# Four head pairs' softmax sums in one group beside a projection, the inverses spread through DRAM, and a new order of transposes and loads

## The chip, the core and the metric

The kernel runs on one core of one Trainium2 chip. The metric is the device time of one execution in microseconds, lower is better. A core has a matrix engine (TensorE, PE in the profile, with its weight loads shown as PEld), a vector engine (DVE), a scalar engine (ACT), GpSimd (POOL, used here to issue loads) and SyncE (SP, used to issue stores, transposes and copies). Each engine works through its own queue in order; they wait for each other by semaphores.

## The reference

Two layers. First an attention with projected keys and values (8 batches, 8 heads, 1024 tokens, head size 64, 64 projected keys), then a feed-forward layer on its output with the square of a ReLU (512 to 2048 to 512).

```python
k_proj = np.einsum('ks,bhsd->bhkd', E, k)
v_proj = np.einsum('ks,bhsd->bhkd', F, v)
scores = scale * np.matmul(q, k_proj.transpose(0, 1, 3, 2))
attn = np.exp(scores - max) / (sum + 1e-09)
x = np.matmul(attn, v_proj)          # then heads side by side: 8192 x 512
out = np.square(np.maximum(x @ w_in, 0.0)) @ w_out
```

## The kernel before

Matmuls are in bf16. The feed-forward layer takes most of the time. Each batch is cut in two chunks of 512 tokens, and both products of a chunk are done by a scheme with seven block products in place of eight (Group for the first layer, Chunk.second_spread for the second), with the sums that it needs on DVE.

After a beginning (batch 0, loads of the weights) comes one main loop of 399 numbered steps (both, L865). A step emits one block product of the first layer (four matmuls of 256 columns, L669) and one quarter product of the second layer of the chunk before (four more, L583). F_STEPS (L833) repeats every seven steps, so a group takes 7 steps, a chunk 28, a batch 56. Steps are counted from 1; firsts of batch 1 are steps 1 to 56, those of batch 2 steps 57 to 112.

The attention of later batches is hung on these steps. on(step, b, name) puts a method of batch b's Attention behind the matmuls of a step (L871 to L901, with t = 56(b-1)+28). TensorE's order is exactly that of the program. The other engines' order is made by a planner when the program is built, from its own estimates of durations; issue_after and add_manual_dep add an order by hand.

One batch's attention consists of these pieces:

- load_kv and load_q (L243 to L248): 1 MB each after the cast to bf16, issued by POOL. K, V and Q have one buffer each, so a load waits until the former batch's tensor has been used.
- project (L266): 16 matmuls with 64 output rows, k's in rows 0 to 63 of one PSUM bank, v's in rows 64 to 127 of the other; then DVE and ACT copy them out (keep_k, keep_v).
- transpose_k_dma and transpose_q_dma (L303, L330): transposes by DMA, issued by SP. qT and kT have one buffer each.
- scores for a head pair (L362): two matmuls of 512 columns, then one Exp on ACT (L353) into one of four expT buffers.
- sums_spread for two head pairs (L386): eight matmuls of 64 rows by 32 columns with a matrix of ones (L392) give the softmax sums, each repeated over 32 rows, of both pairs; Ln and Exp(-x) on ACT (L396, L397) make the inverses; eight copies by DMA within SBUF (L403) repeat them to the 64 rows where they are needed, in two of three "rs" buffers (the third held the source).
- values for a head pair (L406): four matmuls (L415), and two multiplications by rs on DVE (L419) into xT, the input of the first layer.

All attention pieces of the main loop share one pair of PSUM banks (att_psum), so each waits until the piece before has been read out. In the steady state of the loop the order for batch b+2 is: q's transpose at t+26, projection t+28, k's transpose t+30, scores t+44, t+47, (sums t+50), t+53, t+57, (sums t+59), values t+63, t+66, t+76, t+79. K and V of batch b+3 are loaded behind k's transpose (L897), Q of batch b+2 at t+11 behind the last values queued so far (L891). Stores of the output (put, L577) are issued by SP too, from three buffers.

Of the kernel before, what the change touches and what calls it, by code (L numbers as in the profile page):

```python
# [9 lines left out]
P = 128  # L10
F32 = mybir.dt.float32
BF16 = mybir.dt.bfloat16
AF = mybir.ActivationFunctionType
# [6 lines left out]
def kernel(  # L20
# [44 lines left out]
    out_pool = ctx.enter_context(tc.tile_pool(name="outp", bufs=3))  # L65
    psum = ctx.enter_context(tc.tile_pool(name="ps", bufs=1, space=bass.MemoryType.PSUM))
    turn = {"att": 0, "bank": 0, "step": 1, "pairs": 2}

# [6 lines left out]
    def att_psum(shape=(P, 2, TCH), dtype=F32):  # L75
        turn["att"] += 1
        return pair_psum(turn["att"] % turn["pairs"], shape, dtype)
# [149 lines left out]
    for h in half:  # L227
        nc.scalar.copy(kp[:, h].rearrange("p h a d -> p (h a d)"), zeros[:])
    kT = const_pool.tile([P, H, 2, KP], BF16, name="kT")
    VALUE_QUADS = ((LO, 0, 0, LO), (HI, 1, 1, HI), (HI, 0, 1, LO), (LO, 1, 0, HI))  # L230

    class Attention:
# [32 lines left out]

        def project(self):  # L266
            ps = att_psum()
            for i in range(NI):
                f, l = i == 0, i == NI - 1
                nc.tensor.matmul(ps[LO, 0], lhsT=ET[:, i, :], rhs=self.K[:, :, i, :], start=f, stop=l)  # L270
                nc.tensor.matmul(ps[HI, 1], lhsT=FT[:, i, :], rhs=self.V[:, :, i, :], start=f, stop=l)
            self.keep_k(ps[LO, 0], slice(0, H))
            self.keep_v(ps[HI, 1])

        def project_k(self, g):
# [53 lines left out]

        def transpose_q_dma(self):  # L330
            nc.sync.dma_start_transpose(
                self.qT[:].rearrange("p h n t -> p (h n) t"), self.Q[:].rearrange("p h i d -> p (h i d)")
            )

# [50 lines left out]

        def sums_spread(self, pr):  # L386

            ps = att_psum()
            for j in range(2):
                for o, par, a, r in VALUE_QUADS:  # L390
                    c = 32 * (2 * a + j)
                    nc.tensor.matmul(  # L392
                        ps[c:c + 32, par], lhsT=ones[r, 0:32], rhs=self.e[pr + j][r, a], start=True, stop=True
                    )
            inv = soft_pool.tile([P, 2, TCH], F32, tag="rs", name="inv")
            nc.scalar.activation(inv[:], ps[:], AF.Ln)  # L396
            nc.scalar.activation(inv[:], inv[:], AF.Exp, scale=-1.0)  # L397
            for j in range(2):
                rs = soft_pool.tile([P, 2, TCH], F32, tag="rs", name="rs")
                for a in range(2):  # L400
                    have = 32 * (2 * a + j)
                    for to in (64 * a, 64 * a + 32):
                        nc.sync.dma_start(rs[to:to + 32], inv[have:have + 32])  # L403
                self.rs[pr + j] = rs

# [42 lines left out]
    class Chunk:  # L448
# [106 lines left out]
        def keep(self, ps):  # L555
            u = part_pool.tile([P, DM], F32, name="u")
            nc.scalar.copy(u[:], ps)  # L557
            return u
# [9 lines left out]
        def put(self, a, mh, ps, more=None, part=None, o=None):  # L568
# [5 lines left out]
            else:  # L574
                tt(o[:, n], ps, ALU.add, more.rearrange("p (i m) -> p i m", i=2)[:, n])
            i = 4 * self.c + a + 2 * n.start
            nc.sync.dma_start(  # L577
                out_tokens[self.b][:, i:i + 2 * (n.stop - n.start) - 1:2, mh * HM:(mh + 1) * HM], o[:, n]
# [146 lines left out]
    with tc.manual_schedule(engines={PE}):  # L725
# [145 lines left out]
        def on(step, b, name, *args):  # L871
            at(step, lambda: getattr(atts[b], name)(*args))
# [3 lines left out]
        on(12, 1, "chunk_sums", 1, 1)  # L876
        on(15, 1, "chunk_values", 1, 1)
        for b in range(B - 1):
            t = 56 * (b - 1) + 28
            if b:  # L880
                on(t + 1, b + 1, "scores", 3)
                on(t + 3, b + 1, "sums_spread", 2)
                on(t + 7, b + 1, "values", 0)
                on(t + 10, b + 1, "values", 1)
                on(t + 20, b + 1, "values", 2)
                on(t + 23, b + 1, "values", 3)
                at(t + 24, lambda b=b: chunk[b + 1, 0].sum_x())
            at(t + 51, lambda b=b: chunk[b + 1, 1].sum_x())
            if b + 2 < B:
                if b:  # L890
                    on(t + 11, b + 2, "load_q", lambda b=b: atts[b + 1].done)  # L891
                on(t + (26 if b else 32), b + 2, "transpose_q_dma")
                on(t + (28 if b else 36), b + 2, "project")
                on(t + (30 if b else 37), b + 2, "transpose_k_dma")
                if b + 3 < B:
                    at(t + (32 if b else 37), begin, b + 3)
                    on(t + (32 if b else 37), b + 3, "load_kv", lambda b=b: atts[b + 2].kT_done)  # L897
                on(t + (44 if b else 45), b + 2, "scores", 0)
                on(t + (47 if b else 48), b + 2, "scores", 1)
                on(t + (50 if b else 51), b + 2, "sums_spread", 0)  # L900
                on(t + (53 if b else 54), b + 2, "scores", 2)  # L901
        steps = both()
# [33 lines left out]
```

The softmax here doesn't subtract the row's maximum and nothing guards it: scores larger than these inputs give would overflow.

## Time and profile before

| | us |
|---|---|
| median of 3 runs (lowest to highest) | 474.31 (472.84 to 474.36) |
| the profiled execution, whole | 473.11 |
| its span, first to last instruction | 471.3 |
| the main loop: first product to the last windows' end | 72.7 to some 461 |
| q's transpose by DMA: issue, landing | 4.0, 5.6 |
| k's transpose by DMA: issue, landing | 1.2, 2.7 |
| a copy rs<-inv of 128 KB: issue, landing (lowest, median, highest) | 0.59; 2.2, 2.3, 7.8 |
| Ln and Exp of 1024 columns on ACT | 1.02, 1.06 |

Issue is the time that the issuing queue is taken; landing is counted from the start of the issue to the arrival of the data. A profile line of the timeline has the start, the duration, the engine, the line of the program, the operation, what it writes and reads and how many are merged. [...] what a stream of matmuls costs is read from the distance of their starts. In the tables by window the columns are the stretch and its length, then busy time of PE, PEld, DVE, ACT and POOL with the number of instructions, the granted clock, the DMA share and GB/s.

### The profile page before, as it was taken

The numbers are of one execution on the slowest core, as the hardware profiler recorded it, in microseconds if no ns is written. First come the engines' busy times: TensorE is split into PE (matmuls) and PEld (weight loads), VectorE is DVE, ScalarE is ACT, GpSimd is POOL, SyncE is SP. The second block draws the span as 40 slices with busy tenths as digits, with TensorE's granted clock in tenths as the row PEclk, the third lists the DMA queues.
The fourth block names the chain that finished last, engine by engine and source line by source line (L and its number), as shares of the span: only waits on it lengthen the run. The fifth ranks groups of instructions, "written<-read, shape, count | busy, mean of one in ns | idle before, by whom it ended". The sixth has DMA issues, their size and how long they took to land.

```text
span 471.3 us, 10106 instructions
## 1 busy us (share of the span) xinstructions
PE 464.0 (98%) x4123; PEld 367.6 (78%) x4141; DVE 348.1 (74%) x596; ACT 297.7 (63%) x484; POOL 34.0 (7%) x47
## 2 busy tenths in 40 slices
PE   7999999999999999999999999999999999999997
PEld 4544677888888787887888888888878878888886
DVE  2459985876968779667895679777796778968571
ACT  3488595887467863687556775568736875565641
POOL 7430100100010000100001000100000000000000
PEclk9999999999999999999999999999999999999999
DMA  9999998995869578785978848695692154101012
GB/s 182 201 205 207 160 198 177 178 227 114 176 145 210 142 133 200 128 173 131 174 183 146 169 106 174 154 196 156 108 211 88 31 132 107 68 24 68 24 69 89
DMA packets 85743, 67.90 MB, mean 144 GB/s; under 512 B 34368, under 2 KB 82240, under 8 KB 85696
## 3 DMA queue, kind: packets, MB, share of 16 engines
q0 software_dynamic: 32208, 29.23, 40.7%
q1 hardware_dynamic: 53488, 38.02, 30.2%
q8 instruction: 32, 0.52, 0.4%
q14 instruction: 15, 0.12, 0.1%
HBM read 59.24 MB, written 16.78 MB: 161 GB/s over the span
## 4 chain that ended last, share of the span: by engine, by line
PE 97%; DMA 1%; DVE 1%; ACT 1%; issue 0%; SPq 0%; DVEq 0%
PE ps_bank L669 38%; PE ps_second L583 36%; PE ps_bank L502 6%; PE ps_bank L562 4%; PE ps_att L270 3%; PE ps_att L339 2%; PE ps_att L415 2%; PE ps_second L562 1%; DMA k_f<-in_k_dram 1%; PE ps_att L392 1%; PE ps_bank L314 1%; PE ps_bank L220 1%; PE ps_att L349 1%; PE ps_att L345 1%; PE ps_att L289 0%; PE ps_bank L278 0%
## 5 line engine op out<-in xcount | busy, mean ns | idle before, releaser
L154 DVE TENSOR_TENSOR h<-h 128x1024 bf16<-128x1024 bf16 (+1 forms) x170 | 105.4, 645 | 43.9 <-ACT h L679 38.7
L669 PE MATMUL ps_bank<-x_sum,w_in_sum 128*128 128x256 bf16 x672 | 101.1, 273 | 0.1
L669 PEld LDWEIGHTS <-w_in_sum 128*128 128x128 bf16 x896 | 85.4, 98 | 18.9 <-issue 6.3
L583 PEld LDWEIGHTS <-h 128*128 128x128 bf16 x896 | 87.6, 98 | 10.7
L683 DVE CUSTOM_DVE_ANT_0 h<-ps_bank,u 128x512 bf16<-128x512 f32 x112 | 73.8, 685 | 16.2 <-PE ps_bank L669 12.1
L557 ACT COPY u<-ps_bank 128x512 f32<-128x512 f32 x115 | 68.0, 591 | 24.9 <-PE ps_bank L669 23.7
L694 ACT COPY ps_bank<-ps_bank 128x512 f32<-128x512 f32 x56 | 32.0, 571 | 81.5 <-PE ps_bank L669 81.5
L679 ACT ACTIVATE h<-ps_bank 128x512 bf16<-128x512 f32 x112 | 67.9, 607 | 16.7 <-PE ps_bank L669 15.8
L669 PEld LDWEIGHTS <-w_in 128*128 128x128 bf16 x672 | 64.3, 98 | 14.5 <-issue 5.2
L583 PEld LDWEIGHTS <-s 128*128 128x128 bf16 x672 | 65.7, 98 | 7.6
L669 PE MATMUL ps_bank<-xT,w_in 128*128 128x256 bf16 x448 | 67.3, 273 | 0.3
L583 PE MATMUL ps_second<-w_out_sum,s 128*128 128x256 bf16 x448 | 67.2, 273 | 0.0
L583 PE MATMUL ps_second<-w_out_sum,h 128*128 128x256 bf16 x448 | 67.0, 273 | 0.0
L583 PE MATMUL ps_second<-w_out,h 128*128 128x256 bf16 x448 | 64.7, 272 | 0.0
L419 DVE TENSOR_TENSOR xT<-ps_att,rs 128x512 bf16<-128x512 f32 x48 | 30.9, 685 | 13.7 <-PE ps_att L415 13.7
L353 ACT ACTIVATE expT<-ps_att 128x1024 bf16<-128x1024 f32 x32 | 33.1, 1034 | 5.0 <-PE ps_att L339 3.3
L154 DVE TENSOR_TENSOR o_sb<-ps_second,u 128x512 f32<-128x512 f32 x29 | 19.9, 685 | 19.3 <-PE ps_second L583 13.6
L669 PE MATMUL ps_bank<-x_sum,w_in 128*128 128x256 bf16 x224 | 33.7, 273 | 0.3
L669 PE MATMUL ps_bank<-xT,w_in_sum 128*128 128x256 bf16 x224 | 33.6, 273 | 0.1
L583 PE MATMUL ps_second<-w_out,s 128*128 128x256 bf16 x224 | 33.6, 273 | 0.0
L502 PE MATMUL ps_bank<-xT,w_in 128*128 128x512 bf16 x124 | 28.8, 379 | 0.4 <-issue 0.2
L557 ACT COPY u<-ps_second 128x512 f32<-128x512 f32 x30 | 17.6, 586 | 11.6 <-PE ps_second L583 9.3
(96 smaller groups left out, 458.7 us busy)
## 6 DMA issues: line engine op xcount, KB each, us to landing
out_dram<-o_sb SPq DMA_DIRECT2D x63, 256.0 KB, 2.5
rs<-inv SPq DMA_DIRECT2D x96, 128.0 KB, 2.3
K_sb<-in_k_dram POOLq DMA_DIRECT2D x7, 1024.0 KB, 10.0
V_sb<-in_v_dram POOLq DMA_DIRECT2D x7, 1024.0 KB, 14.8
Q_sb<-in_q_dram POOLq DMA_DIRECT2D x6, 1024.0 KB, 12.1
w_out<-in_moe_w_out_dram POOLq DMA_DIRECT2D x4, 512.0 KB, 15.8
Q_sb<-in_q_dram POOLq DMA_DIRECT2D x4, 256.0 KB, 10.9
V_sb<-in_v_dram POOLq DMA_DIRECT2D x2, 512.0 KB, 11.1
```

Source lines behind the costliest of these rows:

```text
L154: return nc.vector.tensor_tensor(out=o, in0=x, in1=y, op=op)
L270: nc.tensor.matmul(ps[LO, 0], lhsT=ET[:, i, :], rhs=self.K[:, :, i, :], start=f, stop=l)
L353: self.done = nc.scalar.activation(e[:], ps[:], AF.Exp, scale=SCALE)
L419: self.done = nc.vector.tensor_tensor(out=self.xT[:, pr, :, par], in0=ps_x[par].rearrange("p (c t) -> p c t", c=2), in1=rs[:, par].rearran ...
L502: nc.tensor.matmul(ps[:], lhsT=w_in_blk(cb, fb), rhs=self.xT[:, cb, self.c].rearrange("p a t -> p (a t)"), start=(cb == 0), stop=(cb == NC ...
L557: nc.scalar.copy(u[:], ps)
L562: nc.tensor.matmul(ps[:, i * HM:(i + 1) * HM], lhsT=self.h_form(n, fb)[:, i * P:(i + 1) * P], rhs=w_out_form(n, fb), start=fresh and fb == ...
L583: nc.tensor.matmul(ps[:, i * HM:(i + 1) * HM], lhsT=self.h_form(n, fb)[:, i * P:(i + 1) * P], rhs=w_out_form(n, fb), start=fresh and i == ...
L669: nc.tensor.matmul(ps[:, j * HC:(j + 1) * HC], lhsT=w_in_form(n, cb, 2 * self.g + j), rhs=self.chunk.x_form(n, cb), start=fresh and j == 0 ...
L679: nc.scalar.activation(self.out(kh, a), ps[:], AF.Relu)
L683: nc.vector._custom_dve(TENSOR_ADD_SAT, out=self.out(kh, a), in0=ps[:], in1=more[:], s0=3.0e38, s1=0.0)
L694: nc.scalar.copy(self.chain[:], self.first[:])
```

## The change

The sums of all four head pairs of a batch are made at once. sums_all adds 16 matmuls of 64 rows by 32 columns into four places: a new constant, pick, holds for pair m ones in the columns 8m to 8m+7 and zeros elsewhere, so that after four accumulated matmuls each place of 32 rows holds the four pairs' sums, each repeated over 8 rows. The places lie in the free quarters of the banks that a projection uses: the projection of batch b+2 and the sums of batch b+1 go into the same pair of banks (project(sums)). For batches 2 and 7 no projection is due there, and sums_alone takes the banks for itself.

ACT then takes Ln over 64 rows for each bank and one Exp over 128 rows, 512 columns each, into a buffer of the pool of u, which has five. SP writes it to DRAM in two stores, and reads it back for each pair in two loads of 64 rows by 4 KB, each with its 8 rows repeated 8 times by the source's access pattern (spread). The spreads of pairs 0 to 2 follow at the next step (batch 2: the same), that of pair 3 after the values of pair 0, behind an out store.

The order changes: q's transpose of batch b+2 stands behind the spread of pair 3 of batch b+1, and the loads of K, V and Q of batch b+3 behind that. In the first turn q of batch 3 is loaded at step 5 and transposed at step 25, and batch 3 is projected at step 34 (before: 39, 54 and 56). The new order for batch b+2 from t: q's transpose t+9, scores t+29, t+36, t+40, t+44, sums with the next projection t+46, spreads t+47, values t+63, t+67, t+73, t+77.

```diff
     psum = ctx.enter_context(tc.tile_pool(name="ps", bufs=1, space=bass.MemoryType.PSUM))
+    dram_pool = ctx.enter_context(tc.tile_pool(name="inv_dram", bufs=2, space=bass.MemoryType.DRAM))
     turn = {"att": 0, "bank": 0, "step": 1, "pairs": 2}
 
     lent = ctx.enter_context(ExitStack())
@@ -227,6 +228,11 @@
     for h in half:
         nc.scalar.copy(kp[:, h].rearrange("p h a d -> p (h a d)"), zeros[:])
     kT = const_pool.tile([P, H, 2, KP], BF16, name="kT")
+
+    pick = const_pool.tile([P, H // 2, 32], BF16, name="pick")
+    nc.scalar.copy(pick[:].rearrange("p m k -> p (m k)"), zeros[:, 0:P])
+    for m in range(H // 2):
+        nc.scalar.copy(pick[:, m, 8 * m:8 * m + 8], ones[:, 0:8])
     VALUE_QUADS = ((LO, 0, 0, LO), (HI, 1, 1, HI), (HI, 0, 1, LO), (LO, 1, 0, HI))
 
     class Attention:
@@ -263,14 +269,20 @@
             nc.scalar.copy(self.vp[HI], view)
             nc.vector.tensor_copy(self.vp[LO], view)
 
-        def project(self):
+        def project(self, sums=None):
             ps = att_psum()
             for i in range(NI):
                 f, l = i == 0, i == NI - 1
                 nc.tensor.matmul(ps[LO, 0], lhsT=ET[:, i, :], rhs=self.K[:, :, i, :], start=f, stop=l)
                 nc.tensor.matmul(ps[HI, 1], lhsT=FT[:, i, :], rhs=self.V[:, :, i, :], start=f, stop=l)
+            if sums:
+                sums.sums_all(ps)
+                sums.log(1)
             self.keep_k(ps[LO, 0], slice(0, H))
             self.keep_v(ps[HI, 1])
+            if sums:
+                sums.log(0)
+                sums.inverse_all()
 
         def project_k(self, g):
             ps = bank()
@@ -327,10 +339,11 @@
                     )
             nc.vector.tensor_copy(self.qT[:, 2 * pr:2 * pr + 2], ps[:])
 
-        def transpose_q_dma(self):
-            nc.sync.dma_start_transpose(
-                self.qT[:].rearrange("p h n t -> p (h n) t"), self.Q[:].rearrange("p h i d -> p (h i d)")
-            )
+        def transpose_q_dma(self, behind=None):
+            with tc.issue_after(atts[behind].spread_done.ins) if behind else nullcontext():
+                self.qT_done = nc.sync.dma_start_transpose(
+                    self.qT[:].rearrange("p h n t -> p (h n) t"), self.Q[:].rearrange("p h i d -> p (h i d)")
+                )
 
 
         def scores_mm(self, ps, pr, n):
@@ -383,25 +396,47 @@
                     nc.vector.tensor_copy(rs[j][lack:lack + 32], rs[j][have:have + 32])
                 self.rs[pr + j] = rs[j]
 
-        def sums_spread(self, pr):
-
-            ps = att_psum()
-            for j in range(2):
+        def sums_all(self, ps=None):
+
+
+            ps = att_psum() if ps is None else ps
+            for m in range(H // 2):
                 for o, par, a, r in VALUE_QUADS:
-                    c = 32 * (2 * a + j)
+                    c = HI.start * (1 - par) + 32 * a
                     nc.tensor.matmul(
-                        ps[c:c + 32, par], lhsT=ones[r, 0:32], rhs=self.e[pr + j][r, a], start=True, stop=True
+                        ps[c:c + 32, par], lhsT=pick[r, m], rhs=self.e[m][r, a],
+                        start=m == 0, stop=m == H // 2 - 1, skip_group_check=True,
                     )
-            inv = soft_pool.tile([P, 2, TCH], F32, tag="rs", name="inv")
-            nc.scalar.activation(inv[:], ps[:], AF.Ln)
-            nc.scalar.activation(inv[:], inv[:], AF.Exp, scale=-1.0)
-            for j in range(2):
-                rs = soft_pool.tile([P, 2, TCH], F32, tag="rs", name="rs")
-                for a in range(2):
-                    have = 32 * (2 * a + j)
-                    for to in (64 * a, 64 * a + 32):
-                        nc.sync.dma_start(rs[to:to + 32], inv[have:have + 32])
-                self.rs[pr + j] = rs
+            self.inv = part_pool.tile([P, TCH], F32, tag="u", name="inv")
+            self.ps_sums = ps
+
+        def log(self, par):
+            rows = (HI, LO)[par]
+            nc.scalar.activation(self.inv[rows], self.ps_sums[rows, par], AF.Ln)
+
+        def inverse_all(self):
+            nc.scalar.activation(self.inv[:], self.inv[:], AF.Exp, scale=-1.0)
+            self.inv_dram = dram_pool.tile([2, H // 2, 8, 2, TCH], F32, name="inv_dram")
+            for par in range(2):
+                nc.sync.dma_start(
+                    self.inv_dram[:, :, :, par].rearrange("a p i t -> (a p i) t"), self.inv[(HI, LO)[par]]
+                )
+
+        def spread(self, pr, behind=None):
+            rs = soft_pool.tile([P, 2, TCH], F32, tag="rs", name="rs")
+            for a, rows in enumerate((LO, HI)):
+                row = self.inv_dram[a, pr].rearrange("i b t -> i (b t)")
+                with tc.issue_after(behind.ins) if behind else nullcontext():
+                    self.spread_done = nc.sync.dma_start(
+                        rs[rows].rearrange("p b t -> p (b t)"), row.unsqueeze(0).broadcast_to((8, 8, 2 * TCH))
+                    )
+            self.rs[pr] = rs
+
+        def sums_alone(self):
+            self.sums_all()
+            self.log(1)
+            self.log(0)
+            self.inverse_all()
 
         def values(self, pr, spare=False):
 
@@ -553,7 +588,7 @@
 
 
         def keep(self, ps):
-            u = part_pool.tile([P, DM], F32, name="u")
+            u = part_pool.tile([P, DM], F32, tag="u", name="u")
             nc.scalar.copy(u[:], ps)
             return u
 
@@ -574,7 +609,7 @@
             else:
                 tt(o[:, n], ps, ALU.add, more.rearrange("p (i m) -> p i m", i=2)[:, n])
             i = 4 * self.c + a + 2 * n.start
-            nc.sync.dma_start(
+            turn["put"] = nc.sync.dma_start(
                 out_tokens[self.b][:, i:i + 2 * (n.stop - n.start) - 1:2, mh * HM:(mh + 1) * HM], o[:, n]
             )
 
@@ -875,30 +910,50 @@
         on(6, 1, "chunk_values", 1, 0)
         on(12, 1, "chunk_sums", 1, 1)
         on(15, 1, "chunk_values", 1, 1)
+        on(4, 2, "transpose_q_dma")
+        at(5, begin, 3)
+        on(5, 3, "load_q")
+        on(8, 2, "project")
+        on(9, 2, "transpose_k_dma")
+        on(10, 3, "load_kv", lambda: atts[2].kT_done)
+        for pr in range(4):
+            on((18, 20, 22, 24)[pr], 2, "scores", pr)
+            if pr < 3:
+                on(26, 2, "spread", pr)
+        plan[26].insert(0, lambda: atts[2].sums_alone())
+        on(34, 3, "project")
+        on(35, 3, "transpose_k_dma")
+        on(25, 3, "transpose_q_dma")
+        at(44, begin, 4)
+        on(44, 4, "load_kv", lambda: atts[2].done)
+        on(44, 4, "load_q", lambda: atts[2].done)
         for b in range(B - 1):
             t = 56 * (b - 1) + 28
-            if b:
-                on(t + 1, b + 1, "scores", 3)
-                on(t + 3, b + 1, "sums_spread", 2)
-                on(t + 7, b + 1, "values", 0)
-                on(t + 10, b + 1, "values", 1)
-                on(t + 20, b + 1, "values", 2)
-                on(t + 23, b + 1, "values", 3)
-                at(t + 24, lambda b=b: chunk[b + 1, 0].sum_x())
             at(t + 51, lambda b=b: chunk[b + 1, 1].sum_x())
+            if not b:
+                continue
+            if b > 1:
+                if b + 2 < B:
+                    at(t - 10, lambda b=b: atts[b + 2].project(atts[b + 1]))
+                    on(t - 9, b + 2, "transpose_k_dma")
+                else:
+                    on(t - 10, b + 1, "sums_alone")
+                for pr in range(3):
+                    on(t - 9, b + 1, "spread", pr)
+                if b + 2 < B:
+                    on(t + 9, b + 2, "transpose_q_dma", b + 1)
+                    if b + 3 < B:
+                        at(t + 12, begin, b + 3)
+                        on(t + 12, b + 3, "load_kv", lambda b=b: atts[b + 2].qT_done)
+                        on(t + 12, b + 3, "load_q")
+            for pr in range(4):
+                on(t + (10, 14, 18, 22)[pr] if b == 1 else t + (7, 11, 17, 21)[pr], b + 1, "values", pr)
+                if pr == 0:
+                    at(t + (10 if b == 1 else 7), lambda b=b: atts[b + 1].spread(3, turn["put"]))
+            at(t + 24, lambda b=b: chunk[b + 1, 0].sum_x())
             if b + 2 < B:
-                if b:
-                    on(t + 11, b + 2, "load_q", lambda b=b: atts[b + 1].done)
-                on(t + (26 if b else 32), b + 2, "transpose_q_dma")
-                on(t + (28 if b else 36), b + 2, "project")
-                on(t + (30 if b else 37), b + 2, "transpose_k_dma")
-                if b + 3 < B:
-                    at(t + (32 if b else 37), begin, b + 3)
-                    on(t + (32 if b else 37), b + 3, "load_kv", lambda b=b: atts[b + 2].kT_done)
-                on(t + (44 if b else 45), b + 2, "scores", 0)
-                on(t + (47 if b else 48), b + 2, "scores", 1)
-                on(t + (50 if b else 51), b + 2, "sums_spread", 0)
-                on(t + (53 if b else 54), b + 2, "scores", 2)
+                for pr in range(4):
+                    on(t + (29, 36, 40, 44)[pr], b + 2, "scores", pr)
         steps = both()
         run(steps)
         assert not plan, plan
```

More of the change, by code (lines that the diff above doesn't have):

```diff
@@ L1 @@
-from contextlib import ExitStack
+from contextlib import ExitStack, nullcontext
 import concourse.bass as bass
```

## The prediction

> **What bounds the kernel now.** I read the page first: busy shares, the slices, the chain that ended last.
>
> ```profile
> PE 464.0 (98%) x4123; PEld 367.6 (78%) x4141; DVE 348.1 (74%) x596; ACT 297.7 (63%) x484; POOL 34.0 (7%) x47
> PEclk9999999999999999999999999999999999999999
> PE 97%; DMA 1%; DVE 1%; ACT 1%; issue 0%; SPq 0%; DVEq 0%
> ```
>
> TensorE is 98% busy at full clock, and the chain runs through it for 97%. Busy time doesn't say whether the matmuls are stretched, so next the table of windows, cut at the projections:
>
> ```profile
> 128.90:184.20 55.30, 55.19 (x504) 45.52 (x504) 42.93 (x72) 35.55 (x59) 2.62 (x3) 1.00 0.78 158
> 184.20:239.60 55.40, 55.29 (x504) 45.58 (x505) 42.96 (x72) 35.64 (x59) 2.62 (x3) 1.00 0.76 158
> ```
>
> Every batch of 56 steps takes 55.3 us, ACT is free for 20 us of it and DVE for 12. Then the TensorE timeline, around one sum and one projection:
>
> ```profile
> 205.53 0.60 PE L669 MATMUL ps_bank<-xT,w_in 128*128 128x256 bf16 x4
> 205.97 0.60 PE L583 MATMUL ps_second<-w_out,s 128*128 128x256 bf16 x4
> 206.50 0.41 PE L392 MATMUL ps_att<-expT,ones 64*32 64x512 bf16 x8
> 206.84 0.61 PE L669 MATMUL ps_bank<-x_sum,w_in_sum 128*128 128x256 bf16 x4
> ...
> 128.55 0.60 PE L583 MATMUL ps_second<-w_out_sum,h 128*128 128x256 bf16 x4
> 129.08 0.40 PE L270 MATMUL ps_att<-K_sb,ET 128*64 128x512 bf16 x1
> ...
> 129.32 0.38 PE L270 MATMUL ps_att<-K_sb,ET 128*64 128x512 bf16 x1
> ...
> 130.93 0.61 PE L669 MATMUL ps_bank<-xT,w_in 128*128 128x256 bf16 x4
> ```
>
> The reader is to see starts, not durations. Four 256-column matmuls follow each other every 0.436 us (205.53 to 205.97), 109 ns each, with no gap: a step of two such fours is 0.873 us. So the loop cannot gain from a wait removed; it gains only from less TensorE work and loses through a new wait. From 205.97 to 206.84 are 0.87 us: less 0.436, the eight sum matmuls cost 0.43. They run side by side as one pass of about 0.216, and 0.2 is lost in change of tile shape: 0.09 going in (206.50 instead of 206.41), about 0.1 coming out. The projection costs 130.93 - 128.55 - 0.436 = 1.94: eight passes of 0.216 and again 0.2.
>
> [...] the spread lands after 2.3 us in quiet, 5.7 us where a q load runs (DMA view, below).
>
> **The change, part by part.**
>
> 1. *TensorE work.* Removed per batch: two sums of 0.43 = 0.87. Added: 16 matmuls on only four tiles (each pair m adds to the same four places), so four passes after each other. Merged with the projection (batches 3 to 6): 4 x 0.216 = 0.86, one more change of shape of 0.1, the way in and out already paid: 0.96, a loss of 0.1. Alone (batches 2 and 7): 0.86 + 0.2 = 1.06, a loss of 0.2. Sum: 4 x 0.1 + 2 x 0.2 = 0.8 us. The passes cannot lie side by side[...]; bounds per batch from -0.55 (four passes as one) to +0.3 (0.1 more per pass at reloading the weights, which L270 doesn't show). I take +0.8 in all.
>
> 2. *ACT.* Removed per batch two Ln of 1.02 and two Exp of 1.06 (by-form groups L396, L397); added two Ln over 64 rows and one Exp over 128, 512 columns each, about 0.6 (L557's copy of 512 columns takes 0.59): 1.8 for 4.2. ACT isn't late anywhere, so its 14 us are worth nothing. Five small copies for pick, an estimated 1.5 us (five below the 0.36 of L259's 256 columns), lie in ACT's first wait for k (3.3 us in the wait list). Cover gone: 1.5.
>
> 3. *Sums to values in later batches.* After step t-10: Ln, copy, Ln, Exp some 3 us; k's transpose on SP ahead of them (1.24 us of issue); two writes to DRAM at 0.6 issue, landing after 2.3 to 2.5 (the out stores land in 2.5); two spreads at 0.6 of issue. One is 64 rows of 4 KB; 32 rows take 2.3 to land[...]. Sum 3 + 1.2 + 1.2 + 2.5 + 1.2 + 3.6 = 12.7 of the 17 steps x 0.873 = 14.8 there are. Not late, 2 us to spare. Loads of the batch after next start behind q's transpose (about step t+17) and take some 22 us, to t+41 at most: off the spreads' path. Behind a late spread DVE's multiply would stand, and behind it all of DVE's queue and TensorE.
>
> 4. *SP and POOL.* Spread 3 sits behind an out store, then q's transpose with 4.1 us of issue and 5.6 to land. It is needed at t+29, 20 steps after; covered. The out stores behind it come up to 5 us later; three buffers against one store in some 6 us cover it.
>
> 5. *First turn, batches 2 and 3.* Here the order is new and tight. SP's and POOL's timelines, then the DMA view of 80 to 110 us; the last line is that of 113 to 127, beside a q load:
>
> ```profile
> 80.35 4.18 SPq L331 DMA_TRANSPOSE qT<-Q_sb  x1
> 84.58 1.30 SPq L304 DMA_TRANSPOSE kT<-kp  x1
> ...
> 87.95 0.87 POOL L89 DMA_DIRECT2D K_sb<-in_k_dram  x1 [18.78 <-DMA kT<-kp]
> 88.82 0.88 POOL L89 DMA_DIRECT2D V_sb<-in_v_dram  x1
> 114.07 0.87 POOL L89 DMA_DIRECT2D Q_sb<-in_q_dram  x1 [24.37 <-DVE xT L419]
> ...
> K_sb<-in_k_dram POOLq DMA_DIRECT2D x1, 1024.0 KB, 9.3
> V_sb<-in_v_dram POOLq DMA_DIRECT2D x1, 1024.0 KB, 14.6
> ...
> rs<-inv SPq DMA_DIRECT2D x5, 128.0 KB, 5.7
> ```
>
> Today K and V of batch 3 are queued at 88 and land at 87.95 + 9.3 = 97.2 and 88.82 + 14.6 = 103.4, 6.2 apart; the projection needs them at 129. After the change Q of batch 3 comes first, as soon as q of batch 2 is transposed (80.35 + 5.65 = 86.0): Q lands at 86.1 + 9.3 = 95.4, K at 101.6, V at 107.8. When is V wanted? Step 17 ends at 90.50 (its score group starts there now); to step 34 are 17 x 0.873 = 14.8, four scores 4 x 0.44 = 1.75, the sums 1.07: 108.1. Into this falls the transpose of q of batch 3, at step 25, from about 98.5 (behind the last scores of batch 2): 1 MB, some 4 us of the same DMA engines. If it waits behind the loads, V lands at 107.8 and nothing is late; if it shares, V comes up to 4 later, at 111.8. I take the middle, 109.8: projection 3 stalls 1.6 us (0 to 3.8), once. V's matmul is the second in TensorE's queue there, and all of the loop stands behind it. The inverses of batch 2, due at step 38 (113.6), queue behind the same transpose: Exp ends about 105, writes land by 110 to 113 under load, the first spread by 115 to 118; with the stall the multiply is wanted at 115.8, and TensorE needs DVE some 2 us after. I take nothing more, and keep 2 us for the range.
>
> **Sum.** 0.8 + 1.6 = 2.4 us. The profiled execution took 473.11 (span 471.3 and 1.8 around it), so 475.5 on that footing; the median of the runs is 474.31, 1.2 above, and I name the time against it: 476.7.
>
> **Rivals.**
>
> - *V lands in time.* Only the 0.8 of TensorE work remains: 475.1, no change that can be told. For it: the store issued beside the q load at 116 landed 9.4 us later, by the DMA view of that stretch, when the load was all but done, so the transpose may queue behind the loads rather than share. Against: three loads in the place of two leave 0.3 us of margin. It decides from V's landing before 108.1. This is the other side.
> - *A stall in every batch.* Scores 3 stand at t+44 and the projection, in the same banks, at t+46, two steps of 1.75 us for an Exp of 1.03 and two handovers of 0.2; and right behind the merged sums ACT has 2.4 us of Ln, copy, Exp ahead of a Relu that the next group's first product waits for (2.6 us after). One ACT instruction of 0.6 in the wrong place costs about 0.5 a batch: five batches 2.5, plus 2.4: 479.2. For it: ACT's order is a planner's. Against: the scores two steps ahead of sums today run with no gap.
> - *The passes overlap.* If the merged sums took two passes instead of four, 6 x 0.43 = 2.6 is gained on the 0.8, and with V in time the result is 474.31 + 0.8 - 2.6 = 472.5, faster. Against: no two matmuls on one tile start closer than 0.216 at 512 columns (129.08, 129.32).
>
> **Numbers.** A measurement of this kernel tells some 0.3% (1.4 us) from no change. Forecast, one stall in the first turn: 0.45; V in time: 0.27; a stall in each batch: 0.20; passes overlap: 0.08. Slower is the forecast, less 0.02 where its stall is under 0.6, and the stall in each batch: 0.63; same 0.29; faster 0.08. The range goes from 474.3 (V in time, passes a little cheaper) to 480.0 (the early stall at its high end, 3.8 + 0.8, or a stall in each batch).
>
> **What would show it.** The merged sums: 16 matmuls in four starts 0.216 apart and 2.9 us for projection and sums together; a start of L270 for batch 3 later than the last of its step by over 0.5 us, with V's landing as its releaser; V of batch 3 landing at about 110; DVE's multiply waiting for the spread in batch 2 alone. Later batches at 55.4 us. Wrong if V lands by 107, if a gap shows at the projections or first products of every batch, or if the spread lands over 6 us after issue in later batches, which would move the wait to DVE.

## The result, and the profile after

| | us |
|---|---|
| before, median of 4 runs (lowest to highest) | 473.57 (472.75 to 474.36) |
| after, median of 4 runs (lowest to highest) | 487.54 (485.09 to 488.39) |
| ratio after to before, 95% interval | 1.0287 (1.0243 to 1.0330) |
| the profiled execution after: whole, span | 488.39, 486.6 |

The changed kernel is slower by 2.9%, some 14 us, where 2.4 were forecast, and the time lies outside the range given (474.3 to 480.0). The page of the kernel after: busy shares, the slices of TensorE and its clock, the chain that ended last by engine and by line, and from the groups DVE's multiply by rs (busy time, mean ns of one, then idle time of the engine before it and what ended most of it):

```profile
PE 469.4 (96%) x4141; PEld 370.8 (76%) x4141; DVE 348.9 (72%) x596; ACT 286.7 (59%) x483; POOL 34.4 (7%) x47
PE   7999999997889998999999999999999999999997
PEclk9999999999799999999999999999999999999999
PE 70%; DMA 13%; DVE 10%; ACT 2%; SPq 2%; issue 2%; DVEq 0%
PE ps_bank L704 25%; PE ps_second L618 24%; DMA rs<-inv_dram 10%; PE ps_bank L537 6%; PE ps_bank L597 4%; PE ps_att L352 3%; DVE h L155 3%; DVE xT L454 2%; PE ps_att L276 2%; DMA inv_dram<-inv 2%; DVE h L718 2%; PE ps_second L597 1%; SPq L430 1%; PE ps_att L406 1%; DMA k_f<-in_k_dram 1%
L454 DVE TENSOR_TENSOR xT<-ps_att,rs 128x512 bf16<-128x512 f32 x48 | 31.3, 684 | 32.7 <-DMA rs<-inv_dram 22.6
```

The number of weight loads is that of before (4141), so no matmuls came in; but the chain, 97% TensorE before, now runs through it for only 70%, and 10% of the span is the spread's transfer, rs<-inv_dram, with DVE behind it. DVE's multiply stood 22.6 us for that spread. The slices place the worst of it: TensorE falls to 7 and 8 in the tenth to twelfth slice (110 to 146 us), and its clock dips in the eleventh. Next the windows of the kernel after, cut at the starts of projections 3, 4, 5, 6 and 7:

```profile
108.68:158.29 49.61, 43.77 (x365) 34.98 (x365) 31.65 (x53) 24.47 (x42) 2.63 (x3) 0.93 0.98 169
158.29:215.34 57.05, 55.62 (x505) 45.79 (x505) 43.07 (x72) 33.48 (x59) 2.63 (x3) 1.00 0.82 151
215.34:271.83 56.49, 55.63 (x506) 45.77 (x505) 43.07 (x72) 33.47 (x59) 2.63 (x3) 1.00 0.85 159
271.83:329.07 57.24, 55.62 (x505) 45.79 (x505) 43.06 (x72) 33.48 (x59) 2.63 (x3) 1.00 0.83 156
```

A batch takes 56.5 to 57.2 us where it took 55.4, at full clock and almost the same busy time (55.6): 1.1 to 1.8 us more in each, nearly all of it gaps. The first turn (projection 3 to projection 4) takes 49.61; almost without stalls it takes 41.1 (a kernel below). TensorE's timeline shows its gap:

```profile
117.68 0.60 PE L704 MATMUL ps_bank<-x_sum,w_in_sum 128*128 128x256 bf16 x4
118.12 0.60 PE L618 MATMUL ps_second<-w_out_sum,s 128*128 128x256 bf16 x4
122.91 0.64 PE L450 MATMUL ps_att<-expT,vp 64*64 64x512 bf16 x4 [4.19 <-DVE xT L454]
123.48 1.03 PE L704 MATMUL ps_bank<-xT,w_in 128*128 128x256 bf16 x4
124.31 1.06 PE L618 MATMUL ps_second<-w_out_sum,s 128*128 128x256 bf16 x4
...
128.42 0.60 PE L704 MATMUL ps_bank<-x_sum,w_in_sum 128*128 128x256 bf16 x4
```

The values of batch 2's second pair wait for the bank that DVE's multiply of the first pair must free. And after the idle 4.2 us the fours start 0.83 to 0.86 us apart, twice the usual 0.436 (the granted clock is 0.50 from 122.9 to 128.24): from 123.48 to 128.42 are 4.94 us for six fours, 2.3 more than 6 x 0.436. The timeline of SP, and the chain in the same stretch:

```profile
99.40 10.37 SPq L344 DMA_TRANSPOSE qT<-Q_sb  x1
...
110.50 1.72 SPq L421 DMA_DIRECT2D inv_dram<-inv  x2
...
114.66 3.84 SPq L430 DMA_DIRECT2D rs<-inv_dram  x6
...
124.45 1.24 SPq L430 DMA_DIRECT2D rs<-inv_dram  x2
```

```profile
111.03 3.58 DMA inv_dram<-inv
...
115.42 6.07 DMA rs<-inv_dram
...
121.56 1.29 DVE xT L454 x2
...
125.11 12.45 DMA rs<-inv_dram
```

Two things lie on top of each other: q's transpose holds SP for 10.4 us ahead of the inverses' stores (which then land in 3.6), and the spreads are slow to land, 6.1 us for the first pair and 12.5 for the last.

In later batches only the second cause is left. What the chain there has of the spreads, DVE's timeline, and the DMA view of the same stretch (busy share of the 16 engines in tenths, then GB/s, in 40 slices of 0.55 us):

```profile
172.08 10.24 DMA rs<-inv_dram
```

```profile
177.10 1.29 DVE L454 TENSOR_TENSOR xT<-ps_att,rs 128x512 bf16<-128x512 f32 x2 [0.85 <-PE ps_bank L704]
182.44 1.29 DVE L454 TENSOR_TENSOR xT<-ps_att,rs 128x512 bf16<-128x512 f32 x2 [4.05 <-DMA rs<-inv_dram]
```

```profile
DMA  5989101164547955354545596994455545554559
GB/s 127 209 199 382 37 0 60 67 223 127 119 119 184 307 119 149 82 149 119 127 119 134 149 289 210 231 135 104 129 130 218 171 149 119 156 119 130 112 172 94
```

The first pair (177.10) waits for nothing from DMA; the second waits 4.05 us. The six spreads of three pairs are issued from 170.1 on, and the DMA view shows traffic again from 172.4 (its ninth slice). From there the share is mostly 4 to 5 tenths, at some 130 GB/s between short peaks; in the first turn, from 116.5 to 118.5, where almost nothing but spreads is on its way, the DMA view gives 45.4% and 135 GB/s. At 130 GB/s four spreads of 256 KB (0.262 MB each) would take 8.1 us, to 180.5, and six 12.1 us, to 184.5. The fourth, the last one that the second multiply needs, was issued at 172.08 and landed at 182.3, between the two. The trace doesn't say in what order the packets of the six were worked off.

### The profile page after: what moved, and what is told of

It reads as the page before. It is cut to its first block, busy times and chain, and to the rows that moved or that the text cites. A ratio compares the mean times of both kernels' runs of the same rounds, so it can differ in the third digit from the quotient of the medians.

```text
span 486.6 us, 10036 instructions
## 1 busy us (share of the span) xinstructions
PE 469.4 (96%) x4141; PEld 370.8 (76%) x4141; DVE 348.9 (72%) x596; ACT 286.7 (59%) x483; POOL 34.4 (7%) x47
## 4 chain that ended last, share of the span: by engine, by line
PE 70%; DMA 13%; DVE 10%; ACT 2%; SPq 2%; issue 2%; DVEq 0%
PE ps_bank L704 25%; PE ps_second L618 24%; DMA rs<-inv_dram 10%; PE ps_bank L537 6%; PE ps_bank L597 4%; PE ps_att L352 3%; DVE h L155 3%; DVE xT L454 2%; PE ps_att L276 2%; DMA inv_dram<-inv 2%; DVE h L718 2%; PE ps_second L597 1%; SPq L430 1%; PE ps_att L406 1%; DMA k_f<-in_k_dram 1%
## 5 line engine op out<-in xcount | busy, mean ns | idle before, releaser
L704 PEld LDWEIGHTS <-w_in_sum 128*128 128x128 bf16 x896 | 86.8, 98 | 22.2 <-issue 8.4
L714 ACT ACTIVATE h<-ps_bank 128x512 bf16<-128x512 f32 x112 | 67.5, 602 | 19.3 <-PE ps_bank L704 17.3
L618 PE MATMUL ps_second<-w_out_sum,s 128*128 128x256 bf16 x448 | 68.4, 276 | 0.0
L454 DVE TENSOR_TENSOR xT<-ps_att,rs 128x512 bf16<-128x512 f32 x48 | 31.3, 684 | 32.7 <-DMA rs<-inv_dram 22.6
L90 POOL DMA_DIRECT2D K_sb<-in_k_dram x9 | 7.8, 865 | 239.0 <-PE ps_bank L704 175.7
```

The costliest lines, as they stand in the source:

```text
L454: self.done = nc.vector.tensor_tensor(out=self.xT[:, pr, :, par], in0=ps_x[par].rearrange("p (c t) -> p c t", c=2), in1=rs[:, par].rearran ...
L618: nc.tensor.matmul(ps[:, i * HM:(i + 1) * HM], lhsT=self.h_form(n, fb)[:, i * P:(i + 1) * P], rhs=w_out_form(n, fb), start=fresh and i == ...
L704: nc.tensor.matmul(ps[:, j * HC:(j + 1) * HC], lhsT=w_in_form(n, cb, 2 * self.g + j), rhs=self.chunk.x_form(n, cb), start=fresh and j == 0 ...
L714: nc.scalar.activation(self.out(kh, a), ps[:], AF.Relu)
```

## The experiments

**1 to 3: width of the spread and place of the transpose.** The theory tried first: while spreads run, the DMA engines are kept only half busy (4 to 5 tenths, 130 GB/s above), and eight spreads, with what follows on SP's queue, become the bound; the rival says that the place of q's transpose does it. e1_spread16 reads four of the eight equal rows 16 times over, so that the outermost dimension is 16 (wide below, "on 16 engines" in the texts on record) and not 8 (narrow); the same bytes land.

```diff
-                row = self.inv_dram[a, pr].rearrange("i b t -> i (b t)")
+                row = self.inv_dram[a, pr, 0:4].rearrange("i b t -> i (b t)")
...
-                        ..., row.unsqueeze(0).broadcast_to((8, 8, 2 * TCH))
+                        ..., row.unsqueeze(0).broadcast_to((16, 4, 2 * TCH))
```

> The changed kernel with one edit: the spread reads 4 of the 8 equal rows and repeats them 16 times, so that its outermost dim is 16 and not 8; same bytes, same number of DMAs. Theory A (the spread keeps to half of the DMA engines, so eight of them take 16 us[...]): its 4 KB packets pass at about 80 per us and not at 32 to 40, q's transpose is issued in about 4 us and not 11, batches 3 to 7 lose nothing, and only part of batch 2's stall stays: 475.5 to 478.5. Theory B (the way through DRAM and the one late group of sums make the inverses late, however many engines carry them): DVE still waits for rs in each batch, 484 to 488.

e2_q_late keeps the narrow spread and puts q of batch 3 behind six spreads; e3_both does both.

```diff
+        on(27, 3, "transpose_q_dma", 2)
-        on(25, 3, "transpose_q_dma")
```

> The changed kernel with one edit: q's transpose of batch 3 stands behind the spreads of batch 2 (step 27) and not ahead of the stores of its inverses (step 25). Theory C (in the first turn the stores of the inverses stood on SP behind that transpose's 10 us of issue, and this is the 4.4 us stall of TensorE at 118 and the clock it loses behind it): the stores are issued at about 105 and not at 110.5, the stall at batch 2's second values goes, the 5 to 6 us of the later batches stay: 480 to 483. If the spread's half of the engines is the whole cause in batch 2 too, the first multiply still waits for 4 us or more: 485 to 488.

> Both edits: spread on 16 engines, q's transpose of batch 3 behind the spreads of batch 2. Theories A and C together: no gap of TensorE over 0.3 us in the main loop; what is left is the 0.8 us of TensorE work that the prediction counted: 474 to 475.5. If something else in the new order costs time (ACT's bursts, the longer stay of K, V, Q loads), 476.5 or more.

| | us | ratio to before (95%) |
|---|---|---|
| after | 487.54 | 1.0287 (1.0243 to 1.0330) |
| e1, spread over 16 | 477.68 | 1.0076 (1.0049 to 1.0103) |
| e2, q late | 495.86 | 1.0457 (1.0429 to 1.0484) |
| e3, both | 475.37 | 1.0026 (1.0008 to 1.0044) |

The width alone takes back 9.9 us, as this theory forecast. The changed kernel's waits for the spread (us in all, times, longest), then e1's, with e1's windows and DMA view:

```profile
DVE xT L454 <- DMA rs<-inv_dram: 22.6, 8, 8.0
```

```profile
DVE xT L454 <- DMA rs<-inv_dram: 5.3, 1, 5.3
```

```profile
108.98:152.36 43.38, 41.12 (x365) 33.50 (x364) 31.31 (x53) 24.16 (x42) 2.62 (x3) 1.00 0.92 191
152.36:207.76 55.40, 55.40 (x506) 45.79 (x505) 43.06 (x72) 33.49 (x59) 2.62 (x3) 1.00 0.78 162
```

```profile
DMA  9100091599799367989979999899738907998999
GB/s 365 48 0 0 0 205 14 246 369 341 246 246 259 82 191 259 410 287 341 232 218 259 219 219 396 171 201 300 280 116 99 160 24 328 437 246 273 225 195 273
...
rs<-inv_dram SPq DMA_DIRECT2D x8, 256.0 KB, 4.9
```

Of eight waits for the spread one is left, in batch 2; a later batch is back at 55.40; the share is mostly at 7 to 9 tenths and the rate some 250 GB/s from the eighth slice on, nearly twice the 130 of the narrow spread. What stands behind the spreads on SP is released too (median issue 5.2 us for 11.4). All issues of q's transpose, in the changed kernel and in e1 (lowest, median, highest ns):

```profile
L344 SPq DMA_TRANSPOSE qT<-Q_sb x6: 4147/11426/11892, 80.7 to 350.9; - x6
```

```profile
L344 SPq DMA_TRANSPOSE qT<-Q_sb x6: 4234/5242/10070, 80.9 to 341.0; - x6
```

The longest in e1, 10.1 us, is that of batch 3, which stands beside the loads of K and V and ahead of the spreads, as in the changed kernel (10.4): there the width changes nothing.

e2 is a miss. The first multiply came in time as foreseen (its wait fell from 7.95 to 2.38 us), but the spread of pair 3 now stood behind a transpose of 12.6 us of issue, and K and V of batch 4 had been queued meanwhile, at 121.6 and 122.5. SP's timeline of e2, its chain, and DVE's timeline:

```profile
112.61 12.60 SPq L344 DMA_TRANSPOSE qT<-Q_sb  x1
...
128.19 1.32 SPq L430 DMA_DIRECT2D rs<-inv_dram  x2
```

```profile
128.92 16.14 DMA rs<-inv_dram
```

```profile
145.15 1.29 DVE L454 TENSOR_TENSOR xT<-ps_att,rs 128x512 bf16<-128x512 f32 x2 [17.18 <-DMA rs<-inv_dram]
```

A transpose put behind slow spreads makes the last spread later still. With the wide spread the same move gains 2.3 us (e1 to e3): the sign of this edit depends on the other. e3's time is as forecast, though one gap is over the 0.3 us that its text allowed: the only one in its first turn, which the prediction had named, the projection's wait for V. Its chain:

```profile
89.33 20.23 DMA V_sb<-in_v_dram
...
109.60 0.38 PE ps_att L277
```

V lands at 109.56 (forecast 109.8) and TensorE stands 0.9 us (forecast 1.6).

**4: one row, 64 copies.** Is it the number of different rows, or the outermost dimension?

```diff
-                row = self.inv_dram[a, pr].rearrange("i b t -> i (b t)")
+                row = self.inv_dram[a, pr, 0:1].rearrange("i b t -> i (b t)")
...
+                        ..., row.unsqueeze(0).broadcast_to((64, 1, 2 * TCH))
```

> As the first of these, but one row is read and repeated 64 times: outermost dim 64, one and the same 4 KB of DRAM read by all. Theory A: only the engines count, so within 1 us of the run with 16 copies of 4 rows, 475.5 to 478.5. If reading the same rows of DRAM many times is what is slow, slower than that run by 3 us or more.

478.77 us, 1.0094 (1.0064 to 1.0123), 1.1 us over e1 and 0.3 over its own range, with intervals that overlap; its spreads land in 3.3, 4.7 and 6.5 us (lowest, median, highest), e1's in 3.2, 4.8 and 6.4. The 3 us that would have spoken against reading the same rows did not come, and reading a quarter of the rows gains nothing: with 16 and with 64 in the outermost dimension the spreads land alike; with 8, in the changed kernel, the chain has 6.1 to 12.5 us.

**5 and 6: sums in two passes.** e5_two_pass takes e3 and makes the sums in a pair of banks of their own with eight places, so that two passes do instead of four; one store takes the inverses, and the projection follows at t-6.

```diff
+            for j in range(2):
+                for u in range(2):
+                    for o, par, a, r in VALUE_QUADS:
+                        c = 32 * (2 * a + u)
...
+                            ps[c:c + 32, par], lhsT=pick[r, j], rhs=self.e[2 * u + j][r, a],
...
-                    at(t - 10, lambda b=b: atts[b + 2].project(atts[b + 1]))
+                on(t - 10, b + 1, "sums_alone")
...
+                    on(t - 6, b + 2, "project")
```

> Both edits, and the sums of the four pairs in banks of their own: eight places, two pairs added to each, so two passes and not four, one store of the inverses; the projection four steps later. Theory: TensorE's work alone sets the loop. The sums cost 0.43 + 0.2 = 0.63 per batch, against 0.87 before and 0.97 to 1.07 in the change, so 1.4 us less than before in six batches; the 0.9 us that projection 3 waits for V in the run with both edits stays: 473.5 to 474.5. If merging with the projection saves what the passes cost, it is slower than the run with both edits.

A miss: 478.53 us, 1.0085 (1.0066 to 1.0105). A later batch takes 55.09 us, as meant, but V of batch 3 landed only at 112.47 (queued 1.3 us later than in e3 and 1.6 longer on its way) and TensorE stood 4.0 us for it, and then ran at half rate. The chain of e5:

```profile
90.62 21.85 DMA V_sb<-in_v_dram
...
113.15 0.37 PE ps_att L277
113.52 0.05 PE ps_att L276
113.58 0.37 PE ps_att L277
```

V's matmuls come 0.43 us apart (113.15 to 113.58) where 0.216 is full rate. e6_kv_first was to load K and V ahead of Q:

```diff
-        on(5, 3, "load_q")
...
+        on(10, 3, "load_q")
```

> As the run before it in this call, and q of batch 3 is loaded behind k and v of batch 3 instead of ahead of them. If the 0.9 us gap before the second matmul of projection 3 is V's place behind Q in the load queue, the gap is gone, V lands 5 to 6 us earlier, and the time is 0.9 less than that run: 472.5 to 473.5, 0.2 to 0.4% under the kernel before. If the gap stays, the cause is the start of K and V, not their place.

477.15 us, 1.0066 (1.0046 to 1.0085). POOL kept the order Q, K, V, since the planner decides it, so this doesn't test what it was meant for. V landed at 110.28, TensorE was idle for 2.4 us, and V's matmuls came 0.43 us apart again.

**7 and 8: K and V really first.** load_q(3) is tied behind V's load, in e7_kv_first on top of e5, in e8_both_kv_first on top of e3.

```diff
+        def load_q_next(self):
+            with tc.issue_after(turn["load"].ins):
+                self.load_q()
...
+        on(10, 3, "load_q_next")
```

> The same with the sums in two passes in banks of their own. Theory: without the wait for V only TensorE's work differs from the kernel before, six times 0.63 against 0.87: 1.4 us less, 472.3 to 473.3. If 474 or more, another wait has taken its place.

> The changed kernel with the spread on 16 engines, q's transpose of batch 3 behind the spreads of batch 2, and q of batch 3 queued on POOL behind v of batch 3 (issue_after, since the run named kv_first left POOL's order as it was). Theory: the wait for V before the second matmul of projection 3 (0.9 to 4 us in the runs with Q first) is V's third place in the queue: V lands at about 104, no gap stays in the main loop, and what is left is the 0.8 us of TensorE work that the prediction counted: 474.5 to 475.5 beside 474.2 of before. If the wait stays, it is the start of the loads.

Both miss: e7 1.0099 (1.0061 to 1.0138), e8 1.0090 (1.0057 to 1.0124); e8 has no usable profile. In e7 V landed at 105.1 and its wait is gone. POOL's timeline, SP's and the chain show what came instead:

```profile
121.74 0.88 POOL L90 DMA_DIRECT2D K_sb<-in_k_dram  x1 [29.19 <-PE ps_second L609]
122.61 0.88 POOL L90 DMA_DIRECT2D V_sb<-in_v_dram  x1
```

```profile
124.20 2.08 SPq L423 DMA_DIRECT2D rs<-inv_dram  x2
```

```profile
124.79 9.76 DMA rs<-inv_dram
```

K and V of batch 4 are queued 2 us ahead of the last spread, which then takes 9.8 us, and TensorE stands 3.1 us for the multiply and soon after 2.0 us for work of DVE behind it.

**9 and 10: the loads of batch 4 behind the spreads.** e9 is e7, e10 is e8, each with

```diff
-        on(44, 4, "load_kv", lambda: atts[2].done)
-        on(44, 4, "load_q", lambda: atts[2].done)
+        on(44, 4, "load_kv", lambda: atts[2].spread_done)
+        on(44, 4, "load_q", lambda: atts[2].spread_done)
```

> As the two-pass run with k and v of batch 3 first, and the three loads of batch 4 wait for the last spread of batch 2 to land, not for the values of batch 2's pair 1. In the run without this they were queued at 121.7 and 122.6, ahead of that spread (124.2), which then took 9.8 us to land and stalled TensorE for 5.8. Theory (a spread that meets a load lands late, whatever else is right): the spread lands within 5 us, the two gaps at 132 and 136 go, and the loop has TensorE's work alone: 472.3 to 473.5 beside 474.2. If it stays at 475 or more, the stall came from q's transpose ahead of the spread on SP.

> The same for the change's own merged sums in four passes: spread on 16 engines, and the first turn's order mended in all three places. The prediction's TensorE sum for the change, 0.8 us, is then all that differs from the kernel before: 474.5 to 475.5. The distance to the two-pass run of this call is the price of four passes and one more change of shape instead of two passes: 0.34 to 0.44 a batch, 2.2 us.

e9 474.19 us, 1.0001 (0.9981 to 1.0020), a miss by 0.7; e10 474.61, 1.0019 (1.0002 to 1.0037), as forecast. No spread takes over 6.4 us to land now. In e9 the first turn still has gaps of 0.38, 0.37 and 1.34 us; the chain leads to the first two from a store of the inverses that took 7.7 us to land beside the load of q, over the first spread and DVE. So e10 lies only 0.4 us above e9, not 2.2: without their gaps (2.1 and 0.46) their main loops differ by 2.0. e10 still has the change's own merged sums in four passes, so it is the changed kernel without its late transfers. Its windows, and its TensorE timeline at one projection:

```profile
107.26:148.36 41.10, 40.70 (x362) 33.29 (x364) 31.49 (x53) 24.14 (x42) 2.63 (x3) 1.00 1.03 200
148.36:203.76 55.40, 55.24 (x503) 45.75 (x505) 43.06 (x72) 33.47 (x59) 2.63 (x3) 1.00 0.80 166
```

```profile
203.23 0.60 PE L622 MATMUL ps_second<-w_out_sum,h 128*128 128x256 bf16 x4
203.76 0.40 PE L280 MATMUL ps_att<-K_sb,ET 128*64 128x512 bf16 x1
...
205.61 1.04 PE L410 MATMUL ps_att<-expT,pick 64*32 64x512 bf16 x16
206.58 0.61 PE L708 MATMUL ps_bank<-xT,w_in 128*128 128x256 bf16 x4
```

Projection and sums cost 206.58 - 203.23 - 0.436 = 2.91 us, where 1.94 + 0.96 = 2.90 were forecast.

**11: a version that beats both.** e11_loads_behind is e9 with each transfer of the first turn in a place of its own: q of batch 3 loaded behind six spreads (step 27) and transposed behind the eighth (step 39), K and V of batch 4 behind that, batch 3's scores at t+33, 37, 41, 44.

```diff
-        on(10, 3, "load_q_next")
+        on(27, 3, "load_q", lambda: atts[2].spread_done)
+        on(39, 3, "transpose_q_dma", 2)
-        on(27, 3, "transpose_q_dma", 2)
...
+        on(44, 4, "load_kv", lambda: atts[3].qT_done)
```

> The two-pass version, with the change's own rule of the later batches also in the first turn: k and v of batch 3 loaded as soon as they can be, q of batch 3 behind the sixth spread of batch 2, its transpose behind the eighth, the loads of batch 4 behind that, and batch 3's scores four, one and one steps later (61, 65, 69). Theory: no spread of batch 2 meets a load except the last pair (7 us to land, wanted 12 us after), so the first turn's gaps of 2.1 us in the run before go and TensorE's work alone is left: 1.4 us under the kernel before, 472.3 to 473.3. If the last pair's landing or q's transpose comes late, a gap of 1 to 4 us shows at batch 2's last values or at batch 3's first scores.

472.60 us, 0.9963 (0.9947 to 0.9979) of before, as forecast: faster than both kernels, though by only 0.4% than the one before. A later batch, by its windows:

```profile
154.06:209.15 55.09, 55.09 (x506) 45.54 (x505) 43.13 (x72) 33.80 (x58) 2.63 (x3) 1.00 0.82 173
```

The stretch is all busy time: 55.09 against 55.36 before, 0.27 a batch from TensorE work alone, with no gap.

## Why the prediction was wrong

**The step that failed** is the last term of step 3's sum, the 3.6 us for a spread to land (2.3 to 5.7 allowed), and with it "Not late, 2 us to spare". The 3.6 was the author's estimate, which no run had shown. The runs show the narrow spread at a share of 4 to 5 tenths and 130 GB/s, against 7 to 9 and some 250 GB/s with the outermost dimension at 16. And the term priced the landing of one spread for the first pair, not the time that the eight of a batch take together: the last spread of the second pair took 10.2 us. Everything ahead of that term held within 1 us: counted from the end of sums 3 in batch 3 (158.29 + 2.9 = 161.2), the first spread was to be issued 7.9 us later, at 169.1, and was issued at 170.10; the first pair was in time. The second pair of the same burst was 4.05 us late. e1 changes that one term, and the waits in later batches are gone.

**Step 5's "I take nothing more"** failed by the same term and one more. The stores of batch 2's inverses did queue behind q's transpose, as the text said, and the first spread, forecast to land by 115 to 118, was only issued at 114.66 and landed at 121.5. What was missing is its 6 us of landing, and that the transpose holds SP for 10.4 us, not 4.1. It did not share with the loads but seems to have waited for them: its issue ended at 109.78, 1.0 us after V landed (108.81), and 1.1 and 0.9 us after V in e1 and e4, where it has the same place. The multiply, wanted at 121.56 - 7.95 = 113.6, came 8 us late. e1 and e2 show that both terms count: the wide spread cuts this wait to 5.3 us, the later transpose to 2.4.

**Where the 14 us are.** The main loop, from its first to its last product of the first layer, takes 382.93 us before and 397.06 after, in e10 383.66. So 0.7 are TensorE's own work and one gap of 0.46 that e10 still has, and 13.4 are late transfers and what they drew after them:

- The first turn has 49.61 - 41.10 = 8.5 us. e10's 41.10 contains a gap of 0.46, so 9.0 are to be explained: gaps of 4.35 and 0.35 at the values of batch 2, 1.8 at 140 us (the last pair's spread, landed at 137.6), and 2.5 of half-rate clock after the long one (the 2.3 above and 0.2 at the values themselves).
- The three batches of the table have 57.05 + 56.49 + 57.24 - 3 x 55.40 = 4.6.
- Batch 7 has 0.4.

The width alone (e1) takes back 6.2 of the first turn and all that the later batches lost.

**What was right.** Step 1, TensorE's work: projection and sums cost what was forecast, and the loop of e10 is +0.7 for +0.8. But 0.46 of it is that gap, so the work itself added some 0.3. Step 2: ACT's 11 us less busy time (297.7 to 286.7, where 14 were counted) are worth nothing.

**Right by luck.** "Slower" was forecast, but for V's stall, which is 0.1 of the 14 us. V was forecast for 109.8 and landed at 108.8 in the changed kernel and at 109.56 in e3, and the stall of 1.6 was 0.1 in the one and 0.9 in the other, within the 0 to 3.8 given. Yet the reason was another one: the 2 us for sharing with q's transpose did not come. V took 19.7, 19.3 and 20.2 us from its issue to landing with that transpose beside it (the changed kernel, e1, e4) and 19.7 and 20.2 without (e2, e3). What made up for it is that Q was queued at 86.96, 0.9 later than forecast, and V came 1.0 later than the 107.8 counted without sharing. The first rival's reading, that the transpose may queue behind the loads, fits better.

**What was off in size.** Step 4 was off in SP's part: q's transpose took a median of 11.4 us of issue where 4.1 was taken, because it stood behind the narrow spreads. The cover was enough all the same; no matmul waited for it.

**The rivals.** A stall in every batch did come, but through the spread and DVE, not through ACT and the projection's bank. The prediction's own list had it, "if the spread lands over 6 us after issue in later batches, which would move the wait to DVE": 10.2 us were seen, and the case was given no time and no chance. Passes that overlap did not come by themselves; e11's two passes are another program.

**Left open.** That in later batches the width of the spread sets how long q's transpose holds SP is shown (11.4 us of issue, median, and 5.2 in e1, which changes nothing else); what in the queue holds it is not, nor is it tested that in the first turn it waits for the loads. Why V took longer in e5 than in e3 was not settled, and e8's first turn was not seen.

## What to carry to other kernels

Price a DMA twice: by how long one takes to land, and by how long all of its kind take together, counted to the last one of the burst; a source that is repeated 8 times in the outermost dimension moved at some 130 GB/s, and the cure was to write the same repetition as 16 by 4, which moved at some 250. What was queued behind slow transfers on the same queue became slow itself (q's transpose: a median of 11.4 us of issue behind narrow spreads, 5.2 behind wide ones), so that moving one of them gained or lost depending on the others (q's transpose of batch 3: -2.3 us beside wide spreads, some +8 beside narrow ones). When a first turn is packed, give each large load a place behind the last small transfer that something waits for, by an explicit order.

## What the runs showed of the hardware

- The issue of a 1 MB transpose by DMA on SP is no constant: 4.0 us in the kernel before, 11.4 (median) behind narrow spreads, 12.6 in e2, 5.2 (median) behind wide ones, and 10.1 to 11.1 beside the loads of K and V (the changed kernel, e1, e4).
- A spread of 256 KB landed in 3.0 to 6.0 us in e11, in up to 9.8 in e7, where two loads were queued 2 us ahead of it, and in 16.1 in e2, narrow and beside two loads.
- After 4.2 us without work TensorE ran at half rate for 5 us (fours 0.85 us apart in place of 0.436; granted clock 0.50 from 122.9 to 128.24, 1.00 after it). Half rate also followed idle gaps of 4.0 us (e5) and 2.4 us (e6), V's matmuls 0.43 us apart behind both, and of 3.1 us (e7, fours 0.85 us apart). Behind 1.75 us (e4), 1.65 us (the changed kernel, at 140 us) and 0.9 us (e3) the rate stayed full. The stall of 4.2 us cost 2.5 us more than itself.
